# Ten output tiles, six shared raw tiles, split GpSimd work and a new schedule in a linear-attention plus token-mixing kernel

**Chip, cores, metric.** One core of one Trainium2 chip. The time is that of the device, in microseconds, the median of several executions. An execution is called slow here when it took over 1.5% more than the fastest of the same kernel; verdicts use the others ("fast"). A ratio is the mean time of one kernel's fast runs over that of the other's fast runs of the same rounds, so it isn't quite the ratio of the medians quoted.

## The reference, cut to what matters

```python
# q, k, v: (8, 8, 576, 64) float32;  w_q, w_k: (512, 64);  w_out: (512, 512)
q_p = concat(relu(q) * cos, relu(q) * sin)        # cos, sin by position
k_p = concat(relu(k) * cos, relu(k) * sin)
kv, z = k_p^T v, sum(k_p)                         # per batch and head
x = (q_p kv) / (q_p z + 1e-6)                     # -> (8, 576, 512)
wq, wk = x w_q, x w_k
mixed = (wq wk^T / 8) x                           # the token mixing
out = relu(mixed) w_out                           # (8, 576, 512) float32
```

## The kernel before

H counts groups of two head pairs, 16 in all: three loads of 576 KB each (q, k, v), GpSimd casts them to bf16 (relu, relu, copy), VectorE multiplies k by the angles (kp), TensorE makes the products, ScalarE and VectorE bring results out of PSUM (the memory that matmuls write). After two groups a batch is whole and its mixing follows (wqk, wk, kx, mx). After two batches come nine output projections (wo), each with a copy from PSUM into an output tile (oe) and two stores of 128 KB (st). The order of the instructions on every engine is decided ahead of time by a list scheduler with a small model of costs and waits. The parts concerned:

```python
inp = ctx.enter_context(tc.tile_pool(name="inp", bufs=4))          # for each of q, k, v
outpool = ctx.enter_context(tc.tile_pool(name="outpool", bufs=4))
...
raw[nm, H] = inp.tile([P, 2, HC], FP32, name=f"{nm}f")
...
def wout_evac(bp, rt, m, eng):
    o_sbs[bp, rt] = outpool.tile([P, DM], FP32, name="o_sb")
    copy(eng, o_sbs[bp, rt], bank(m)[:, 0, :])
...
# in the scheduler: loads know their buffers, output copies (oe) do not
op(("load", nm, H), {"DMA": 1.51}, [ago(H > 4, "r" + nm, H - 4)])
op(("oe", p, rt), {"ACT": .60, "DVE": .71}, [("wo", p, rt)], par["poe"], ...)
op(("st", p, rt), {"DMA": .67}, [("oe", p, rt)])
...
elif kind == "rq":
    relu_q(b, 0, C9, G)          # one GpSimd instruction for a whole tensor
elif kind == "st":
    last = b == B // 2 - 1 and j >= 4
    store(b, j, (nc.sync, A if last else nc.sync))   # nearly all on SP, as the loads
```

## Time and profile before

| | before |
|---|---|
| time, median of 3 | 144.14 us (144.09 to 145.95) |
| span of the profiled run, mean granted clock (share of TensorE's full clock) | 141.7 us, 0.892 |
| busy PE / DVE / ACT / POOL | 111.5 / 97.9 / 80.2 / 64.2 us |
| ACT and DVE waiting for stores | 8.6 + 5.8 us |
| kp multiply, mean | 1.726 us |
| store, issue to landing, median / worst | 3.0 / 10.7 us |

No engine is busy throughout, and the DMA engines are full for the first 88 us only.

### The profile page before, as it was taken

The page shows a single profiled execution, that of the slowest core. Times are in us where ns is not written, and L with a number is a line of the kernel's source. Part 1 is how long each engine was busy: PE and PEld are TensorE (multiplying, and loading weights), DVE is VectorE, ACT ScalarE, POOL GpSimd, SP SyncE. Part 2 cuts the span into 40 slices and gives each one's busy share as a digit, 9 for nine tenths or more (in the row PEclk, how much of TensorE's full clock was granted, in tenths as well). Part 3 has the DMA queues.
Part 4 walks back from the last instruction along what each step waited for, and adds up shares of the span by engine and source line. Part 5 has one row for each costly group of instructions (what it writes and reads, how often), then busy time and mean ns, then how long its engine had stood idle before and what let it go on. Part 6 is the DMA issues. An engine that isn't in the chain of part 4 may idle for free.

```text
span 141.7 us, 5312 instructions
## 1 busy us (share of the span) xinstructions
PE 111.5 (79%) x2257; PEld 66.1 (47%) x2279; DVE 97.9 (69%) x148; ACT 80.2 (57%) x159; POOL 64.2 (45%) x76
## 2 busy tenths in 40 slices
PE   5857688697999581897979479998899799989920
PEld 2334356476565330545545335664665564533300
DVE  1167994999949921679899946999989776365200
ACT  6930175377758650337846096487877766644340
POOL 7747837985898995065575603656100000000000
PEclk9999968965599959559999987999999999999995
DMA  4999999999999999999999999553333703857874
GB/s 111 374 389 390 347 384 390 392 388 391 392 389 391 387 389 401 398 395 396 400 398 387 395 297 385 132 124 76 77 79 79 153 2 76 186 113 153 179 212 127
DMA packets 21239, 39.40 MB, mean 278 GB/s; under 512 B 3040, under 2 KB 4576, under 8 KB 21216
## 3 DMA queue, kind: packets, MB, share of 16 engines
q1 hardware_dynamic: 20544, 38.08, 80.2%
q10 hardware_dynamic: 672, 0.98, 2.3%
q8 instruction: 18, 0.29, 0.9%
q14 instruction: 5, 0.04, 0.1%
HBM read 29.62 MB, written 9.44 MB: 276 GB/s over the span
## 4 chain that ended last, share of the span: by engine, by line
DMA 51%; PE 19%; issue 9%; DVE 7%; ACT 4%; POOL 3%; ACTq 2%; SPq 1%; POOLq 0%; DVEq 0%
DMA qf<-in_q_dram 13%; DMA kf<-in_k_dram 12%; PE ps L526 10%; DMA wo_f<-in_moe_w_out_dram 9%; DMA wq_f<-in_moe_w_q_dram 8%; DMA vf<-in_v_dram 6%; DMA out_dram<-o_sb 3%; ACT o_sb L329 2%; PE ps L416 2%; DVE qpt_buf L383 2%; ACTq L536 2%; POOL rk L342 2%; PE ps L456 1%; PE ps L502 1%; PE ps L486 1%
## 5 line engine op out<-in xcount | busy, mean ns | idle before, releaser
L526 PE MATMUL ps<-wo_sb,mix_sb 128*128 128x512 bf16 x125 | 37.5, 404 | 4.3 <-issue 1.8
L355 DVE TENSOR_TENSOR kp<-rk,cossin 128x2304 bf16<-128x2304 bf16 (+2 forms) x17 | 27.4, 1613 | 10.0 <-ACT rk L340 5.9
L329 ACT COPY o_sb<-ps 128x512 f32<-128x512 f32 x34 | 20.0, 588 | 23.2 <-PE ps L526 13.4
L342 POOL TENSOR_SCALAR rq_buf<-qf 128x1152 bf16<-128x1152 f32 (+2 forms) x17 | 20.6, 1214 | 18.2 <-PE ps L377 10.2
L367 POOL TENSOR_SCALAR v_buf<-vf 128x1152 bf16<-128x1152 f32 x15 | 20.6, 1375 | 14.8 <-PE ps L391 11.7
L429 DVE TENSOR_TENSOR x_sb<-ps,rec 128x640 bf16<-128x640 f32 x32 | 26.4, 824 | 1.1
L383 DVE TENSOR_TENSOR qpt_buf<-ps,cst 128x1152 bf16<-128x1152 bf16 x32 | 22.6, 747 | 0.0
L416 PEld LDWEIGHTS <-qpt_buf 64*128 64x128 bf16 x640 | 15.1, 99 | 15.0 <-issue 13.9
L526 PEld LDWEIGHTS <-mix_sb 128*128 128x128 bf16 x144 | 12.5, 102 | 17.2 <-issue 6.9
L416 PE MATMUL ps<-kv_sb,qpt_buf 64*128 64x65 bf16 x320 | 17.0, 199 | 3.8 <-DVE x_sb L429 3.4
L342 POOL TENSOR_SCALAR rk<-kf 128x1152 bf16<-128x1152 f32 x15 | 19.0, 1270 | 1.5 <-DMA kf<-in_k_dram 1.4
L416 PE MATMUL ps<-kv_sh,qpt_buf 64*128 64x65 bf16 x320 | 17.1, 198 | 1.1
L329 ACT COPY xT_buf<-ps 128x512 bf16<-128x512 bf16 (+1 forms) x24 | 15.1, 643 | 2.8 <-PE ps L441 2.2
L391 PE MATMUL ps<-v_buf,kp 64*128 64x65 bf16 x576 | 14.2, 199 | 3.1 <-DVE qpt_buf L383 3.1
L514 ACT ACTIVATE mix_sb<-ps 128x576 bf16<-128x576 f32 x24 | 15.0, 652 | 2.3 <-PE ps L502 2.1
L391 PEld LDWEIGHTS <-kp 64*128 64x128 bf16 x576 | 11.8, 100 | 7.4 <-issue 3.3
L456 PE MATMUL ps<-xT_buf,wqk_sb 128*128 128x288 bf16 x64 | 10.3, 303 | 5.0 <-DVE xT_buf L331 4.3
L329 ACT CAST kv_sb<-ps 128x260 bf16<-128x260 f32 x14 | 5.3, 378 | 14.3 <-PE ps L391 14.1
L427 DVE RECIPROCAL rec<-ps 128x10 f32<-128x10 f32 x32 | 6.8, 214 | 8.6 <-PE ps L420 8.4
L502 PE MATMUL ps<-wT_buf,kx 64*128 64x288 bf16 x32 | 9.2, 311 | 3.3 <-ACT kx L329 2.7
L252 PE MATMUL ps<-warm 128*128 128x512 bf16 x28 | 9.7, 485 | 2.1 <-DVE warm L248 1.5
L329 ACT CAST wT_buf<-ps 128x576 bf16<-128x576 f32 x8 | 5.1, 639 | 8.9 <-PE ps L456 8.9
(51 smaller groups left out, 122.3 us busy)
## 6 DMA issues: line engine op xcount, KB each, us to landing
qf<-in_q_dram SPq DMA_DIRECT2D x15, 576.0 KB, 10.5
kf<-in_k_dram SPq DMA_DIRECT2D x15, 576.0 KB, 9.7
vf<-in_v_dram SPq DMA_DIRECT2D x15, 576.0 KB, 9.6
out_dram<-o_sb SPq DMA_DIRECT2D x67, 128.0 KB, 3.1
wo_f<-in_moe_w_out_dram SPq DMA_DIRECT2D x1, 1024.0 KB, 12.1
out_dram<-o_sb ACTq DMA_DIRECT2D x5, 128.0 KB, 2.8
kf<-in_k_dram ACTq DMA_DIRECT2D x1, 320.0 KB, 4.3
qf<-in_q_dram SPq DMA_DIRECT2D x1, 320.0 KB, 4.0
```

The source lines that it names most:

```text
L329: nc.scalar.copy(dst, src)
L342: eng.tensor_scalar(dst, src, FMAX, 0.0, op0=ALU.min, op1=ALU.max)
L355: nc.vector.tensor_mul(kp[H][:, 2 * lo:2 * hi], rks[H][:, lo:hi].rearrange("p c i d -> p (c i) d").unsqueeze(2) .to_broadcast([P, 2 * (hi ...
L367: eng.tensor_scalar(dst, src, 1.0, 1.0, op0=ALU.mult, op1=ALU.mult)
L383: nc.vector.tensor_mul(qpt_bufs[H % 2][:, r, :, D:SLOTS * D], bank_h(K0 + r)[:, 0:1, 0:HC].to_broadcast([P, 2, HC]), cst)
L391: nc.tensor.matmul(bank(K0 + r)[:, 0, i * (D + 1):(i + 1) * (D + 1)], kp[H][half_rows(r), 2 * c + i, :, :], v_bufs[H % 3][half_rows(r), c, ...
L416: nc.tensor.matmul(nb[t][:, u, :], qpt_bufs[H % 2][rows, r, w, u * P:(u + 1) * P], mv, start=(u == 0 and w == 0), stop=False)
L429: nc.vector.tensor_tensor(xv[:, h, r], nv[:, :, :, 0:D], rec.to_broadcast([P, 2, SC, D]), op=ALU.mult)
L456: nc.tensor.matmul(bank(m + nh)[:, 0, 0:hs], wqk_sb[:, dmc, :, :], xT_bufs[b % 2][:, dmc, nh * hs:(nh + 1) * hs], start=(dmc == 0), stop=( ...
L502: nc.tensor.matmul(bank(m + r)[:, 0, 0:hs], kxs[b][half_rows(r), i * P:(i + 1) * P], rhs, start=True, stop=True)
L514: nc.scalar.activation(dst, src, AF.Relu, scale=scale_moe)
L526: nc.tensor.matmul(bank(m)[:, 0, :], mixs[bp][:, dmc, rt * P:(rt + 1) * P], wo_sb[:, dmc, :], start=(dmc == 0), stop=(dmc == NDM - 1))
```

## The change

Its intent: output tiles enough that no copy out of PSUM waits for a store; fewer loads in the queue ahead of a store; GpSimd pieces short enough that VectorE is not held long; and a scheduler that knows these limits. Cut to its core:

```diff
-PLAN = dict(mk=1.5, pa=3.218, pc=3.9, pm=3.2, pw=1.86, pb=0.0, flex=.163, poe=4.5, ...
+PLAN = dict(mk=1.5, pa=7.057, pc=7.377, pm=6.4, pw=5.394, pb=0.0, flex=.249, poe=3.15, ...
+            pmk=.82, wo_at=4, nraw=6, nout=10)
-                op(("load", nm, H), {"DMA": 1.51}, [ago(H > 4, "r" + nm, H - 4)])
+                i = 3 * H + "qkv".index(nm) - par["nraw"]
+                op(("load", nm, H), {"DMA": 1.51},
+                   [ago(i >= 3, "r" + "qkv"[i % 3], i // 3)])
-            op(("oe", p, rt), {"ACT": .60, "DVE": .71}, [("wo", p, rt)], par["poe"],
+            i = 9 * p + rt - par["nout"]
+            op(("oe", p, rt), {"ACT": .60, "DVE": .71},
+               [("wo", p, rt), ago(i >= 0, "st", i // 9, i % 9)], par["poe"],
+                elif e == "DMA":
+                    key = t          # a transfer is placed when it is ready,
+                                     # not when the modelled DMA is free
-        done[n] = s + c + after[e]
+        done[n] = s + c + (1.6 if n[0] == "st" else after[e])
-    inp = ... bufs=4            +    inp = ... bufs=PLAN["nraw"]     (name="raw" for all three)
-    outpool = ... bufs=4        +    outpool = ... bufs=PLAN["nout"]
-            relu_q(b, 0, C9, G)
+            for lo, hi in CS:                  # (0, 5), (5, 9); the same for k and v
+                relu_q(b, lo, hi, G)
```

More of the change, by code (lines that the diff above doesn't have):

```diff
@@ L21 @@
 EPS_HI = 9.9837780e-07
-PLAN = dict(mk=1.5, pa=3.218, pc=3.9, pm=3.2, pw=1.86, pb=0.0, flex=.163, poe=4.5, pme=3.3,
-            pmk=.7, wo_at=4)
+PLAN = dict(mk=1.5, pa=7.057, pc=7.377, pm=6.4, pw=5.394, pb=0.0, flex=.249, poe=3.15, pme=3.3,
+            pmk=.82, wo_at=4, nraw=6, nout=10)
 def plan_order(NB, par=None):
@@ L204 @@
     consts = ctx.enter_context(tc.tile_pool(name="consts", bufs=1))
-    inp = ctx.enter_context(tc.tile_pool(name="inp", bufs=4))
+    inp = ctx.enter_context(tc.tile_pool(name="inp", bufs=PLAN["nraw"]))
     prep = ctx.enter_context(tc.tile_pool(name="prep", bufs=2))
@@ L210 @@
     mixpool = ctx.enter_context(tc.tile_pool(name="mixpool", bufs=2))
-    outpool = ctx.enter_context(tc.tile_pool(name="outpool", bufs=4))
+    outpool = ctx.enter_context(tc.tile_pool(name="outpool", bufs=PLAN["nout"]))
     psum = ctx.enter_context(tc.tile_pool(name="psum", bufs=1, space=bass.MemoryType.PSUM))
@@ L237, in load @@
         for nm in names:
-            raw[nm, H] = inp.tile([P, 2, HC], FP32, name=f"{nm}f")
+            raw[nm, H] = inp.tile([P, 2, HC], FP32, name="raw")
         for lo, hi in parts:
@@ L556, in emit @@
         elif kind == "rq":
-            relu_q(b, 0, C9, G)
+            for lo, hi in CS:
+                relu_q(b, lo, hi, G)
         elif kind == "rk":
-            relu_k(b, 0, C9, G)
+            for lo, hi in CS:
+                relu_k(b, lo, hi, G)
         elif kind == "rv":
-            cast_v(b, 0, C9, G)
+            for lo, hi in CS:
+                cast_v(b, lo, hi, G)
         elif kind == "mk":
```

## The prediction

> **What bounds the kernel now.** I read the page's slices first, then busy time by stretch, then the waits, then the timeline around the longest wait, then the loads at the SP queue.
>
> The slices of the page:
>
> ```profile
> PE   5857688697999581897979479998899799989920
> DVE  1167994999949921679899946999989776365200
> POOL 7747837985898995065575603656100000000000
> PEclk9999968965599959559999987999999999999995
> DMA  4999999999999999999999999553333703857874
> ```
>
> A slice is 3.54 us. The DMA row is full from slice 1 to 24 (to about 88 us) and half empty after. Loads are 29.6 MB; at some 392 GB/s (the page's GB/s row in those slices) they need 75.5 us, and the stores that go out meanwhile fill the rest. So the loads do set the pace at first. But PE and DVE both have a hole in slices 14 to 16 (50 to 60 us) and a second at 23 (81 to 85 us), while DMA is full. Those holes are not hunger for data. After 88 us another 54 us pass with no loads at all: compute has a debt, and the time is set by when that debt is paid.
>
> Busy time by stretch (us; PE, PEld, DVE, ACT, POOL; then granted clock, DMA share, GB/s):
>
> ```profile
> 50.00:57.00 7.00, 3.54 (x26) 1.43 (x26) 1.22 (x3) 1.81 (x6) 5.03 (x5) 0.74 1.05 396
> 57.00:65.00 8.00, 7.07 (x127) 4.38 (x127) 5.48 (x10) 2.91 (x7) 2.64 (x3) 0.61 1.04 394
> 65.00:80.00 15.00, 12.70 (x334) 8.14 (x337) 14.32 (x21) 9.50 (x21) 8.87 (x8) 1.00 1.05 396
> 80.00:90.00 10.00, 7.28 (x137) 4.19 (x140) 6.62 (x10) 6.39 (x13) 3.06 (x4) 0.83 0.89 310
> 90.00:130.00 40.00, 36.68 (x777) 21.89 (x783) 31.76 (x53) 27.42 (x55) 7.08 (x6) 1.00 0.48 102
> ```
>
> From 65 to 80 DVE is 95% busy, from 90 to 130 PE is 92% busy: there compute is the bound and runs well. From 50 to 57 DVE works 1.2 us of 7, and the 8 us after it run at a clock of 0.61.
>
> What the holes wait for, from the table of waits (total us, times, longest):
>
> ```profile
> ACT o_sb L329 <- DMA out_dram<-o_sb: 8.6, 4, 3.9
> DVE o_sb L331 <- DMA out_dram<-o_sb: 5.8, 1, 5.8
> POOL v_buf L367 <- PE ps L391: 11.7, 6, 4.6
> POOL rq_buf L342 <- PE ps L377: 10.2, 5, 5.2
> ```
>
> The first two say that a copy into an output tile had to wait for an older store to land. The other two say that GpSimd, and so the loads, runs ahead of compute and is held by it, not the reverse. The timeline:
>
> ```profile
> 45.13 4.90 SPq L536 DMA_DIRECT2D out_dram<-o_sb  x4
> 50.64 1.06 PE L526 MATMUL ps<-wo_sb,mix_sb 128*128 128x512 bf16 x2 [0.22 <-issue]
> 56.23 0.69 DVE L331 COPY o_sb<-ps 128x512 f32<-128x512 f32 x1 [5.78 <-DMA out_dram<-o_sb]
> 56.89 0.59 ACT L329 COPY o_sb<-ps 128x512 f32<-128x512 f32 x1 [3.89 <-DMA out_dram<-o_sb]
> 57.37 1.84 PE L456 MATMUL ps<-xT_buf,wqk_sb 128*128 128x288 bf16 x7 [3.60 <-DVE xT_buf L331]
> 60.50 1.15 POOL L342 TENSOR_SCALAR rq_buf<-qf 128x1152 bf16<-128x1152 f32 x1 [5.22 <-PE ps L377]
> 81.21 0.59 ACT L329 COPY o_sb<-ps 128x512 f32<-128x512 f32 x1 [3.42 <-DMA out_dram<-o_sb]
> ```
>
> Four output tiles were filled by 47 us; their stores were issued only from 45.13. The fifth tile takes the first one's buffer, so its copy on DVE, whose matmul was done at 51.7, sits until 56.2 with all later DVE work behind it; then ACT, then PE, then GpSimd. For the stores of this tile the trace gives, issue to landing:
>
> ```profile
> DMA to landing us min/median/max: 2.2/3.0/10.7
> ```
>
> 45.13 + 10.7 is 55.8: the slowest store is the one waited for. It is slow because some seven loads of 1.5 us each lie before it (loads land 9.6 to 10.5 us after issue).
>
> **What the Trainium skill says.** "DMA: Bandwidth & Descriptors", section "Queues, rings and completion order": SP's transfers use one row of rings, and each engine consumes descriptors in ring order. Here loads and nearly all stores are on SP, so a store waits out the loads ahead of it; the trace agrees (10.7 us amid loads, 2.2 us at the least). "SBUF — State Buffer", section "Who interferes with whom": a VectorE instruction with two SBUF inputs and a GpSimd instruction that reads SBUF exclude each other for a whole instruction. The kp multiply has two SBUF inputs; the trace has it at 1.35 us alone and 2.33 us when it starts at 86.34, just behind a GpSimd cast of 86.32, so it agrees. "TensorE: Matmul & The Clock Gate", section "What's actually happening": the clock is halved after an idle window of about 3.4 us and restored by a busy one. The idle 3.60 us of PE before 57.37 and the clock of 0.61 after it agree.
>
> **The change part by part.**
>
> Ten output buffers. A tile lives from its copy to the landing of its store, at worst about 5 us in the SP queue plus 10.7. Tiles come about once in 2.5 us in this phase (36 in some 90 us), so six or seven can be alive; four are too few and ten are enough. It takes away:
> 1. First stall: DVE could have copied at 51.7 instead of 56.2: 4.5 us.
> 2. The cold clock after it: 7.07 us of PE work at 0.61 would need 0.39 x 7.07 = 2.8 us less; PE is not alone on the path there, so I count half, 1.4.
> 3. Second stall: ACT waits 3.4 us at 77.8 to 81.2, PE idles 2.7 us for it (before 82.13). I count 2.7, and for the clock of 0.83 in 80 to 90, half of 0.17 x 7.28: 0.6.
> 4. The last tiles: two copies wait 0.65 us each for a store, but most of that is ACT issuing its own store (0.5 us each). I count 0.5.
>
> GpSimd in two pieces. Now 15 kp multiplies average 1.726 us against 1.35 alone: 5.6 us lost; 8 wq copies average 0.543 against 0.303: 1.9. A piece of 640 takes 0.72 us (first q piece, uncontended), a whole 1152 takes 1.15. A line through both gives 0.18 us fixed and 0.61 for a piece of 512, so a pair costs 1.33, 0.18 more, and 45 tensors cost 8 us more of an engine that is 45% busy. A VectorE operation then waits for half as long a piece: about half of 7.5 us, 3.8, is saved on DVE. DVE is the bound in about 45% of the kp multiplies (65 to 80 and 90 to 100 us): 1.7 us.
>
> Raw buffers. Twelve become six. One is being worked on, so at most five loads are in flight: 5 x 1.5 = 7.5 us of queue, against a lone-transfer time of some 4 us (the first loads land after 4.0 to 4.7). That keeps DMA full while GpSimd keeps up, and a store waits at most 7.5 us instead of 10.7. It removes nothing from the path by itself, and takes away slack.
>
> The scheduler's limits and weights change the order on every engine; I can't size this from the profile and put it at 0, in the range only.
>
> Gross sum: 4.5 + 1.4 + 2.7 + 0.6 + 0.5 + 1.7 = 11.4 us.
>
> What is given back: the last v tensor is cast at 98.55 now. With some 10 us gained by then it could be at 88.5. But its load was issued at 82.97 and landed about 87, and in a faster kernel the five output tiles of 88 to 98 us (1.3 MB, 3.3 us at 392 GB/s) go ahead of it: about 90. So some 1.5 us come back as a wait for the load. The raw buffers' lost slack I put at another 0.3. 144.1 - 11.4 + 1.5 + 0.3 = 134.5; call it 134.
>
> **The rivals.**
>
> A: the loads become the bound again. Six buffers shared in order mean that one late GpSimd piece holds all three kinds. In the early stretch (10 to 50 us) GpSimd was busy 31.4 of 40 us; with 0.18 us more for each of its 25 tensors it is 36 of 40, that is 1.44 us for each tensor against 1.5 for its load. With waits for q and v buffers on top, DMA would show gaps before 80 us. For it: the margin is 4%. Against: with compute unstalled the 10.2 and 11.7 us of GpSimd waits mostly vanish. It would give back 3 to 5 us: 137 to 139.
>
> B: DVE is the next bound. It is busy 97.9 us, all but a few of them between 8 and 130 us, so freed output tiles help only until DVE is 95% busy. For it: 65 to 80 us. Against: 8.6 us of it idles for numerators, and the contention falls. It would leave 6 us of gain: 138.
>
> C: it goes better than the sum. PE did 23 us of full-clock work by 45 us (busy times clock, by stretch) and 67 from there to 136.6. In 90 to 130 it reached 92% of the time. At 88% throughout, 67 us take 76, and the end comes at 121 plus some 7 us of last stores and launch: about 128. For it: the order was tuned anew with truer limits. Against: loads cannot supply head pairs so early.
>
> D: nothing is gained, because the copies wait for something else (PSUM banks, PE). Against: both holes end at a landing store within 0.5 us.
>
> **Range and chances.** A and B pull to 137 to 139, C to 128; the sum lies between. Predicted 134.0 us, 8 in 10 between 128.5 and 139.5. The threshold for faster by 2% is 141.3: all rivals but D lie below it. Faster 0.91, within 2% 0.07, slower 0.02.
>
> **What would show it.** Waits of ACT and DVE for stores gone or under 2 us (now 14.4); no hole in DVE in slices 14 to 16; clock 0.9 or more from 50 us on; kp multiply near 1.5 us; GpSimd some 72 us busy; GpSimd's waits for PE down by half and waits for loads up; DMA full to about 85 us; the time after the last load below 46 us. It is wrong if DMA has gaps before 80 us with SP waiting for GpSimd (rival A), if DVE stays over 95% busy without the contention falling (B), or if the store waits are gone and the same holes stand there for another reason (D).

## The result, and the profile after

133.88 us (median of 4 executions, 132.46 to 136.10) against 144.23 us: a ratio of 0.916, 95% interval 0.905 to 0.928. Two executions are fast (132.46, 132.56, clock 0.97), two are slow (135.19, 136.10, clock 0.95). The profiled one is fast.

The slices of the changed kernel, now 3.27 us each:

```profile
PE   5947685885699989986999699889947999899930
DVE  1065979689994999959999987989659876346200
PEclk9999999999959999999999999999999999999995
DMA  3999999999999999999999999999974034837973
```

The hole of slices 14 to 16 is gone from DVE and PE. The clock dips in one slice (35.9 to 39.2 us) and at the very end, where before there were ten such slices and the end. DMA stays full until about 95 us and 36 us follow, not 54: the debt is smaller.

Its waits (total us, times, longest):

```profile
ACT o_sb L335 <- DMA out_dram<-o_sb: 0.9, 2, 0.6
POOL rq_buf L348 <- DMA raw<-in_q_dram: 7.9, 6, 2.9
POOL v_buf L373 <- DMA raw<-in_v_dram: 6.6, 10, 0.8
POOL v_buf L373 <- PE ps L383: 0.5, 1, 0.5
```

The waits for stores fell from 14.4 to 0.9 us. GpSimd waited 21.9 us for TensorE; now it waits for loads. The timeline around the place of the first stall:

```profile
39.76 1.18 SPq L542 DMA_DIRECT2D out_dram<-o_sb  x2
42.17 1.10 SPq L542 DMA_DIRECT2D out_dram<-o_sb  x2
49.74 0.68 DVE L337 COPY o_sb<-ps 128x512 f32<-128x512 f32 x1
50.12 0.58 ACT L335 COPY o_sb<-ps 128x512 f32<-128x512 f32 x1 [0.34 <-PE ps L532]
```

Two things differ from before, and these lines alone can't say which counts. The fifth copy (49.74) has a buffer of its own. But the first store also left at 39.76, not 45.13, since the new order puts it ahead of loads that stood before it. The experiments separate them.

### The profile page after: what moved, and what is told of

It is laid out like the page before. It is cut to its first block, busy times and chain, and to the rows that moved or that the text cites. A ratio compares the mean times of both kernels' runs of the same rounds, so it can differ in the third digit from the quotient of the medians.

```text
span 130.8 us, 5363 instructions
## 1 busy us (share of the span) xinstructions
PE 105.8 (81%) x2279; PEld 61.8 (47%) x2279; DVE 93.8 (72%) x153; ACT 78.5 (60%) x154; POOL 76.8 (59%) x121
## 4 chain that ended last, share of the span: by engine, by line
PE 43%; DMA 23%; DVE 14%; ACT 5%; POOL 5%; issue 4%; SPq 2%; ACTq 1%; POOLq 0%
PE ps L532 19%; DMA raw<-in_k_dram 12%; DMA raw<-in_q_dram 9%; PE ps L422 5%; PE ps L462 5%; PE ps L397 5%; DVE kp L361 4%; DVE qpt_buf L389 4%; PE ps L492 3%; POOL rk L348 3%; PE ps L447 2%; PE ps L383 2%; DVE x_sb L435 2%; PE ps L508 2%; POOL rq_buf L348 2%
## 5 line engine op out<-in xcount | busy, mean ns | idle before, releaser
L348 POOL TENSOR_SCALAR rq_buf<-raw 128x640 bf16<-128x640 f32 (+1 forms) x32 | 26.2, 835 | 9.3 <-DMA raw<-in_q_dram 7.9
L373 POOL TENSOR_SCALAR v_buf<-raw 128x640 bf16<-128x640 f32 (+1 forms) x30 | 27.1, 920 | 7.4 <-DMA raw<-in_v_dram 6.6
L361 DVE TENSOR_TENSOR kp<-rk,cossin 128x2304 bf16<-128x2304 bf16 (+2 forms) x17 | 22.5, 1324 | 11.3 <-ACT rk L346 6.1
L335 ACT COPY o_sb<-ps 128x512 f32<-128x512 f32 x32 | 18.8, 586 | 15.8 <-PE ps L532 12.9
L348 POOL TENSOR_SCALAR rk<-raw 128x640 bf16<-128x640 f32 (+1 forms) x30 | 19.5, 669 | 4.2 <-DMA raw<-in_k_dram 2.7
L335 ACT COPY xT_buf<-ps 128x640 bf16<-128x640 bf16 (+1 forms) x25 | 15.7, 650 | 3.0 <-PE ps L447 1.7
L397 PE MATMUL ps<-v_buf,kp 64*128 64x65 bf16 x576 | 13.1, 190 | 3.8 <-DVE qpt_buf L389 2.9
L397 PEld LDWEIGHTS <-kp 64*128 64x128 bf16 x576 | 10.6, 94 | 8.2 <-issue 3.4
L383 PE MATMUL ps<-ident,rq_buf 64*128 64x64 bf16 x288 | 8.1, 192 | 2.6 <-POOL rq_buf L348 1.3
L462 PE MATMUL ps<-xT_buf,wqk_sb 128*128 128x288 bf16 x64 | 9.2, 287 | 0.0
```

The costliest lines, as they stand in the source:

```text
L335: nc.scalar.copy(dst, src)
L348: eng.tensor_scalar(dst, src, FMAX, 0.0, op0=ALU.min, op1=ALU.max)
L361: nc.vector.tensor_mul(kp[H][:, 2 * lo:2 * hi], rks[H][:, lo:hi].rearrange("p c i d -> p (c i) d").unsqueeze(2) .to_broadcast([P, 2 * (hi ...
L373: eng.tensor_scalar(dst, src, 1.0, 1.0, op0=ALU.mult, op1=ALU.mult)
L397: nc.tensor.matmul(bank(K0 + r)[:, 0, i * (D + 1):(i + 1) * (D + 1)], kp[H][half_rows(r), 2 * c + i, :, :], v_bufs[H % 3][half_rows(r), c, ...
L462: nc.tensor.matmul(bank(m + nh)[:, 0, 0:hs], wqk_sb[:, dmc, :, :], xT_bufs[b % 2][:, dmc, nh * hs:(nh + 1) * hs], start=(dmc == 0), stop=( ...
```

## The experiments

Each ran beside the kernel before on one chip. Before took a median of 144.23 us in the changed kernel's own job, 143.83 in that of e1 to e4, 144.32 in that of e5 to e8 and 145.04 in that of e9 to e12.

| run | what | median us | ratio of fast runs (95%) |
|---|---|---|---|
| changed kernel | | 133.88 | 0.916 (0.905 to 0.928) |
| e1 | before + ten output tiles | 133.02 | 0.921 (0.912 to 0.930) |
| e2 | before + GpSimd in pieces | 144.27 | none: one fast run |
| e3 | before + six shared raw tiles | 145.58 | 1.007 (1.000 to 1.015) |
| e4, e10 | before + all three, old order | 132.91, 133.94 | 0.918, 0.925 |
| e5 | changed, four output tiles | 137.41 | none: one fast run, 133.24 |
| e6 | before, stores placed early | 148.02 | 1.026 (1.018 to 1.034) |
| e7 | changed, twelve raw tiles | 134.20 | 0.928 (0.920 to 0.937) |
| e8 | changed, whole GpSimd tensors | 134.23 | 0.929 (0.920 to 0.937) |
| e9 | changed, again | 133.79 | 0.922 (0.916 to 0.927) |
| e11 | before + six output tiles | 137.29 | 0.946 (0.939 to 0.954) |
| e12 | e10 + VectorE copies in the tail | 132.86 | 0.915 (0.908 to 0.921) |

The theory: a copy into an output tile that waits for a landing store stops its engine and everything behind it, and this alone is what the change removes. Rivals: the new order; the depth of the load queue; the contention of VectorE and GpSimd.

### e1: ten output tiles and nothing else

```diff
-    outpool = ... bufs=4
+    outpool = ... bufs=10
```

> The kernel before with ten output buffers and nothing else. Theory (the stalls on landing stores are the cost, any order that is not stalled will do): the sum's terms 1 to 4, 9.7 us less, minus 1.5 for loads that come later: 134 to 137 us; waits of ACT and DVE for stores fall from 14.4 us to under 2. Rival (the new order of instructions is what gains): the holes close but others open, at most 3 us gained: 141 us or more.

133.02 us: as far as these runs resolve it, the whole gain comes from this one number. (The table of waits still puts 2.8 us to stores. With each copy matched to its two stores by their order, the stores that free those four tiles had landed 11 us or more earlier, so no copy waits for a tile any more.) As every engine's order is that of the kernel before, the same instruction can be followed through both traces. The cast that ends each batch's wqk stage, the third to the fifth and the last of eight, before:

```profile
59.24 0.64 ACT L329 CAST wT_buf<-ps 128x576 bf16<-128x576 f32 x1 [1.77 <-PE ps L456]
74.56 0.64 ACT L329 CAST wT_buf<-ps 128x576 bf16<-128x576 f32 x1 [1.86 <-PE ps L456]
90.84 0.64 ACT L329 CAST wT_buf<-ps 128x576 bf16<-128x576 f32 x1 [1.65 <-PE ps L456]
123.89 0.64 ACT L329 CAST wT_buf<-ps 128x576 bf16<-128x576 f32 x1 [0.35 <-PE ps L456]
```

and with ten tiles:

```profile
54.79 0.64 ACT L329 CAST wT_buf<-ps 128x576 bf16<-128x576 f32 x1 [0.39 <-PE ps L456]
67.87 0.64 ACT L329 CAST wT_buf<-ps 128x576 bf16<-128x576 f32 x1 [0.95 <-PE ps L456]
80.88 0.64 ACT L329 CAST wT_buf<-ps 128x576 bf16<-128x576 f32 x1 [1.65 <-PE ps L456]
113.43 0.64 ACT L329 CAST wT_buf<-ps 128x576 bf16<-128x576 f32 x1 [0.44 <-PE ps L456]
```

The second cast was 1.34 us later in e1 (42.65 against 41.31), before any tile was short. So 4.45 us are gained across the first stall, or 4.45 + 1.34 = 5.8 counted from that later start (whether those 1.34 us would have been made up without the stall isn't shown), 6.69 - 4.45 = 2.2 in the stretch after it, 9.96 - 6.69 = 3.3 across the second stall, and 0.5 from there to the last. Gains lie where the stalls were, and little comes after 91 us. The stores themselves are as slow as ever: the worst takes 10.7 us here too. It is no longer waited for.

The same matching of copies and stores gives how long a tile lives, from the start of its copy to the landing of its second store, and how many are alive when a copy starts:

| run | tiles | longest life, us | most alive |
|---|---|---|---|
| before | 4 | 17.9 | 4 |
| e11, before + six tiles | 6 | 19.4 | 6 |
| e1, before + ten tiles | 10 | 20.0 | 9 |
| e3, before + six shared raw tiles | 4 | 18.4 | 4 |
| e4, all three, old order | 10 | 24.2 | 10 |
| changed kernel | 10 | 12.0 | 5 |
| e5, changed, four tiles | 4 | 10.0 | 4 |

Ten tiles suit the old order, which uses nine or ten. The new order shortens the life and never has more than five alive.

### e2 and e8: the two GpSimd pieces, added alone and taken away alone

```diff
 # e2, on the kernel before; e8 is the reverse on the changed kernel
-            relu_q(b, 0, C9, G)
+            for lo, hi in CS:
+                relu_q(b, lo, hi, G)          # likewise k, v
```

> The kernel before with GpSimd's work in two pieces and nothing else. Theory: the kp multiply falls from 1.726 to about 1.4 us, GpSimd's busy time rises by 8 to 13 us, but both stalls on stores stand, so 0 to 2 us are gained: 142 to 144 us. Rival (contention of VectorE and GpSimd is the main cost): 4 us or more gained, under 140 us.

> The changed kernel with GpSimd's work in whole tensors again. Theory (the pieces save some 2 to 4 us of VectorE that lie mostly beside other work): the kp multiply goes from 1.40 to about 1.6 us, GpSimd from 76.8 to about 66 us busy, and the time rises by 0 to 2 us: 132 to 136 us. Rival (pieces matter once the stalls are gone and VectorE is the bound): 137 us or more.

e2: 144.27 us, with one execution at 141.62 and three at 143.98 to 145.49, so no verdict beyond "about the same". The stalls stand (16.1 us of waits for stores). e8: 134.23 us, against 133.88 and 133.79 for the changed kernel; the intervals overlap. The multiply itself, before, by form:

```profile
L355 DVE TENSOR_TENSOR kp<-rk,cossin 128x2304 bf16<-128x2304 bf16 x15 | 25.9, 1726 | 4.1 <-POOL rk L342 2.0 <-PE ps L391 1.8
```

In the changed kernel:

```profile
L361 DVE TENSOR_TENSOR kp<-rk,cossin 128x2304 bf16<-128x2304 bf16 x15 | 21.0, 1400 | 5.2 <-POOL rk L348 5.2
```

Here 4.9 us of VectorE busy time are saved, for 76.8 - 64.2 = 12.6 us more on GpSimd. But the same kernel in e9, in a fast execution too, has

```profile
L361 DVE TENSOR_TENSOR kp<-rk,cossin 128x2304 bf16<-128x2304 bf16 x15 | 24.0, 1598 | 2.8 <-POOL rk L348 2.8
```

Whole tensors have 1.516 us in e1 and 1.511 in e8 (a slow execution), pieces alone 1.520 in e2. So one profile of each doesn't show what the pieces save. Nor is it resolved what reaches the end: e8's ratio is 0.007 to 0.013 above those of the changed kernel, 1 to 2 us, within the intervals.

### e3: six shared raw tiles alone

```diff
-    inp = ... bufs=4                        +    inp = ... bufs=6
-            raw[nm, H] = inp.tile(..., name=f"{nm}f")
+            raw[nm, H] = inp.tile(..., name="raw")
 # and each load is held back in program order until its buffer's last reader stands before it
```

> The kernel before with six shared raw buffers, each load put at the first place at which its buffer's reader stands before it, all other engines' order kept, four output buffers. Theory: a store waits behind five loads at most, its worst landing falls from 10.7 to about 7.5 us, and each of the two stalls shrinks by about 3 us: 138 to 141 us. Rival A (six are too few): DMA shows gaps before 80 us and the time is 144 us or more.

A miss for the theory's number: 145.58 us, no gain. The worst store now lands in 7.2 us, as expected, and yet neither stall is shorter (the second grew from 3.4 to 5.4 us), and the tiles live as long as before. The time is what rival A gave, but not its sign: DMA has no gap before 80 us. The profiled execution is the slow one of four, 146.79 us, and is used only for where the waits lie:

```profile
48.67 2.45 SPq L536 DMA_DIRECT2D out_dram<-o_sb  x4
56.31 0.69 DVE L331 COPY o_sb<-ps 128x512 f32<-128x512 f32 x1 [5.90 <-DMA out_dram<-o_sb]
```

The store left at 48.67, not 45.13. The loads ahead of it no longer wait in the DMA rings; they wait at SP for GpSimd to free a buffer, and the store waits behind them there. SP's own waits for GpSimd, by the tensor it was freeing:

```profile
SPq L242 <- POOL v_buf L367: 16.4, 9, 5.9
SPq L242 <- POOL rq_buf L342: 15.7, 13, 2.0
SPq L242 <- POOL rk L342: 7.2, 9, 1.1
```

A shallower queue moved the wait from behind SP to in front of it. Fewer loads in flight didn't help here, because the store still stood behind them in SP's program order.

### e6: stores placed right after their copies

```diff
     for n, eng, m in plan_order(NB):
+        if n[0] == "st":
+            continue
         emit(n, eng, None if m is None else M0 + m)
+        if n[0] == "oe":
+            emit(("st",) + n[1:], None, None)
```

> The kernel before, with four output buffers, but each store placed at the SP queue right after its copy in program order, ahead of the loads that the scheduler had put before it. Theory (the life of an output tile is its place in the SP queue plus the ring, and only that life counts): the first store goes out about 40.5 us, not 45.13, its buffer is free about 51 us, just when it is wanted, and half or more of the gain comes without a buffer: 134 to 139 us. Rival (the ring of loads in the DMA engines is what holds stores, the place at SP counts little): 141 us or more.

A clear miss: the store waits vanish (0.6 us left) and the time rises to 148.02 us. SP's queue shows why:

```profile
26.66 0.42 SPq L242 DMA_DIRECT2D kf<-in_k_dram  x1
40.02 2.81 SPq L536 DMA_DIRECT2D out_dram<-o_sb  x4
42.92 0.54 SPq L242 DMA_DIRECT2D vf<-in_v_dram  x1
```

SP issues nothing from 27 to 40 us. It stands at a store whose copy is not yet made (its longest wait for a ScalarE copy is 12.6 us); the three loads behind it go out at once when it moves on. From 36 to 40 us the DMA engines are 27% busy, and later VectorE waits:

```profile
36.00:40.00 4.00, 3.97 (x50) 1.93 (x45) 3.75 (x6) 2.47 (x4) 3.74 (x3) 0.50 0.27 101
```

```profile
DVE kp L355 <- POOL rk L342: 19.4, 9, 4.6
POOL v_buf L367 <- DMA vf<-in_v_dram: 12.7, 12, 3.2
```

(The first fence is the stretch's row by engine, then clock, DMA share and GB/s; the second is from the table of waits.) A wait removed by putting its cause first became a wait of the loads. The old scheduler places loads late in program order, when its modelled DMA gets free; so "right after the copy" is ahead of loads that were due long ago. My expectation took the loads that stood before the store in time for loads that stood before it in the program.

### e5 and e4, e10: the order without the tiles, the tiles without the order

```diff
 # e5, on the changed kernel (the plan still assumes ten)
-    outpool = ... bufs=PLAN["nout"]
+    outpool = ... bufs=4
```

> The changed kernel with four output buffers in place of ten, its order of instructions and all else kept. Theory (ten buffers alone carry the gain): the waits of ACT and DVE for stores come back, 8 us or more in total, and the time is 139 to 144 us. Rival (the scheduler's new order, with stores placed earlier among the loads at the SP queue, avoids the stalls by itself): waits under 3 us, 132 to 136 us.

> Ten outputs, six shared raw buffers and two pieces, with the order of the kernel before (loads delayed as in the run before). Theory: all the sum's terms but the order, which the prediction put at 0: 132 to 136 us. Rival (the order carries half of the gain): 138 us or more.

> All buffers and pieces with the order of the kernel before, again. Theory: 131 to 134 us, within 1 us of the changed kernel, in either direction. Rival: 134.5 us or more.

> The changed kernel once more, beside the next two on one chip. Fast executions at 132 to 134 us, some 1.5 to 3 us longer as in the first job. Theory (once the tiles are there the order is worth nothing): its fast executions are within 1 us of those of the next run. Rival (the order still gains): 1.5 us or more below it.

e5 surprised me: its fast execution took 133.24 us with four tiles, and its trace has 1.7 us of waits for stores:

```profile
40.29 1.52 SPq L542 DMA_DIRECT2D out_dram<-o_sb  x2
51.30 0.68 DVE L337 COPY o_sb<-ps 128x512 f32<-128x512 f32 x1
```

The first store leaves at 40.29, the fifth tile is wanted at 51.30, eleven microseconds later, and by then the store has landed (it takes 5.0 us; the worst of this run takes 8.5). So the new order, with the pieces and shared raw tiles that it came with, can do without ten tiles what the tiles do, in the one fast execution seen. The order without those two wasn't run. The other three executions took 136.99 to 137.83 us. The changed kernel has slow executions too (135.19 and 136.10 in its own job, 136.14 and 137.87 in e9), but they are four of ten. That four tiles leave e5 less slack may be, and is not shown: no trace of its slow executions was taken.

The reverse is e4 and e10: tiles, pieces and shared buffers with the old order, 0.918 and 0.925. Beside e10 on the same chip the changed kernel (e9) has 0.922. With the tiles there, the order adds nothing that these runs resolve.

### e7: twelve raw tiles in the changed kernel

```diff
-    inp = ... bufs=PLAN["nraw"]             +    inp = ... bufs=4
-            raw[nm, H] = inp.tile(..., name="raw")
+            raw[nm, H] = inp.tile(..., name=f"{nm}f")
```

> The changed kernel with four raw buffers for each of q, k and v again, same order at every engine. Theory: six shared buffers neither gain nor cost beyond 1.5 us, since GpSimd's waits for loads at the end come from stores that share the DMA engines: 131 to 136 us; the loads' landing goes from 7.2 back to about 10 us. Rival (six are too few and the late last loads at 93 to 97 us are theirs): the last v cast starts 3 us or more earlier and the time is under 131 us.

134.20 us, 0.928 (0.920 to 0.937), the same within the intervals. Six shared tiles save memory, and no time is seen to be lost or gained. One detail of the expectation is a miss: with twelve tiles the loads land in 7.3 to 7.7 us (medians), not about 10, so in the new order it isn't the six tiles that keep the queue short.

### e11: six output tiles

```diff
-    outpool = ... bufs=4
+    outpool = ... bufs=6
```

> The kernel before with six output buffers and nothing else. Theory (a tile lives 10 to 16 us while tiles are wanted every 2 to 4 us, so six to seven cover it): the waits for stores fall to 2 to 5 us in total and 133 to 137 us is reached, most of the gain of ten. Rival (all ten are needed): 138 us or more.

137.29 us, just outside what the theory gave, and a miss for the waits: 7.6 us in place of 2 to 5.

```profile
ACT o_sb L329 <- DMA out_dram<-o_sb: 7.6, 5, 3.1
```

Six bring about two thirds of the gain (0.946 against 0.921 for ten). Three of these five copies (6.4 us of waits) start just after the landing of the stores that free their buffer; so does a VectorE copy that the table puts to a load (1.9 us, at 82.23). My "six or seven can be alive" took a life of 15.7 us and a mean rate. In e1 a tile lives up to 20.0 us, as its first store leaves SP up to 13.8 us after the copy starts, not 5, and nine are alive at once. The trace of the kernel before had shown it: the third tile's copy starts at 44.32, its first store leaves at 55.50.

### e12: can it be beaten?

```diff
-            wout_evac(b, j, m, engs[eng])
+            tail = b == B // 2 - 1 and j in (5, 7)
+            wout_evac(b, j, m, V if tail else engs[eng])
```

> As the run with all buffers and the old order, and of the last five output tiles two are copied by VectorE, which has nothing else to do there. Theory: ScalarE's period of 1.2 us for a copy and the issue of a store is what sets the last five tiles; TensorE needs 0.97, so about 1 us is gained: 130 to 133 us, a ratio to the kernel before lower by about 0.007. Rival (the last store's landing or TensorE sets the end): no change.

132.86 us, 0.915 (0.908 to 0.921), beside 0.925 (0.919 to 0.932) for e10, the same kernel without the edit, and 0.922 for the changed kernel. The first copy of the last five to the last copy takes 124.80 - 120.28 = 4.5 us, in e10 127.07 - 121.78 = 5.3. Over all six executions the means are 132.89 and 134.08. The gain fits the expected microsecond, but the intervals still touch; it is the best of these kernels by its median beside the others, not by a settled margin.

## Why the prediction was right

It gave 134.0 us and 133.88 came. The cause was right and is shown by e1. The closeness is partly luck: 133.88 is the median of two fast and two slow executions, the fast ones took 132.5, and the sum itself came to 134.5. By its own steps:

- **First and second stall, with the clock after them.** Summed at 4.5 + 1.4 + 2.7 + 0.6 = 9.2 us. e1's aligned casts show 10.0 by the fifth cast, or 5.8 + 2.2 + 3.3 = 11.3 from the later start: the place and the cause are right, the size 0.8 to 2.1 us too small. The second stall is exact (2.7 + 0.6 for 3.3). The stretch after the first stall (2.2 us) is the term that I halved to 1.4. Whether the cold clock made it isn't shown. As a whole the mean clock predicts little: executions of the kernel before at 0.905 and 0.938 took 143.22 and 143.24 us.
- **The last tiles.** 0.5 us predicted, nothing found at the two copies that it named: they waited 0.65 us each for a store, and wait 0.63 and 0.62 with ten tiles, now put to ScalarE's own work. The 0.5 us that e1 gains between the fifth batch's cast and the last lie before them.
- **GpSimd in pieces.** 3.8 us less VectorE work predicted; on kp 4.9 in one profile of the changed kernel and 1.9 in the other (e9). Of the 1.7 us put on the path, none is resolved (e2, e8). GpSimd is busy 76.8 us, not 72: a pair takes 1.30 us when alone (1.33 worked out), and many pairs take longer beside VectorE, up to 2.5.
- **What is given back.** 1.8 us predicted for late loads and lost slack. In e1 the last v cast starts at 90.54, where I had said about 90, for 98.55 before; the end still comes 11.1 us of span earlier. The load was waited for, and no loss of it shows at the end (that TensorE had projections to do meanwhile would explain it). In the changed kernel the cast starts at 96.93, only 1.6 us before 98.55, and the end comes 10.9 us earlier: the last cast doesn't set the end as this step assumed. The 1.8 us not paid and the 1.7 us not seen cancel.
- **The order, put at 0.** As an addition to ten tiles that holds (e9, e10). As a cause it was too simple: e5 removes the same stalls without the ten tiles in its fast execution, and the table under e1 shows how, by a shorter life. Order and tiles are substitutes, and their gains don't add.
- **Rival A** (loads bound again) did not come: DMA is full to 95 us. Its margin was misread: the trace has 23 GpSimd tensors from 10 to 50 us, not 25, so (31.45 + 23 x 0.18) / 23 = 1.55 us each against 1.5 for a load. **B** (VectorE next) did not: it is busy 93.8 us of 130.8. **C** (about 128) was not reached, and its sum was short: from 45 to 136.6 us the trace has 70 us of full-clock work, not 67, which at 88% and with the 7 us gives about 132. **D** falls with e1.

One step of the reasoning was wrong though no number hung on it: that a shallower load queue shortens the wait of an output tile. e3 shows that the life stays the same (18.4 us at the longest, 17.9 before).

## What to carry to other kernels

When a copy waits for its output tile, follow that tile from copy to landing and count what stands ahead of its store in the issuing queue's program order. Here shortening the ring behind the queue, or pushing the store ahead of loads already due, only moved the wait. Count the tiles alive at once from the trace rather than from mean rates: nine in e1, five in the new order. More tiles are the simple cure: one number, with the order left as it was. Two cures for one stall don't add: test each alone and undo each alone before crediting either.

## What the Trainium skill lacked or had wrong

- "DMA: Bandwidth & Descriptors", section "Specifications", gives about 358 GB/s as the limit of HBM for one core. Here loads and stores ran at 393 GB/s on average from 20 to 80 us of the kernel before, with one core in use. The section "Bandwidth" of the same page does mark its own single-core figures as such, up to 425 GB/s, and gives about 358 for each core when both of a pair stream.
- "DMA: Bandwidth & Descriptors", section "Anatomy of one DMA — SWDGE (gpsimd) path", says that a DMA's wait is done by the issuing sequencer before dispatch. No page read here says what follows for mixed loads and stores: a store that waits for its data holds the loads behind it. Measured in e6: SP issued nothing from 27 to 40 us, DMA fell to 27%, and the kernel lost 2.6%.
- "TensorE: Matmul & The Clock Gate", section "What's actually happening", has the clock halved after an idle window and restored by one busy window of about 3.4 us. In the kernel before the trace has a granted clock of 0.50 from 30 to 38 us, with TensorE busy 6.96 of those 8 us by its records, and again from 50 to 52; between 8 and 53 us TensorE had no idle gap over 0.9 us. So the idle gap of 3.60 us that the prediction points to fits only the low clock after 57. Either busy in the trace is not the activity that the gate counts, or the rule isn't whole; these runs don't show which.
